# Layer norm, sliding attention and a Mish FFN on one core: additions ahead of the attention step, fixed PSUM banks, an interleaved start

## The chip, the core and the metric

The kernel runs on one core of a Trainium2 chip. The metric is the device time of one execution in microseconds. TensorE (PE) multiplies, VectorE (DVE), ScalarE (ACT) and GpSimd (POOL) do the elementwise work, SyncE (SP) issues the DMAs. Results of matmuls land in PSUM, of which the kernel holds eight banks of 128 x 512 fp32 values, four named h and four named out; everything else lies in SBUF, and what does not fit there is parked in DRAM.

## The reference

The input x has 2048 tokens of 576 features; all is fp32.

```python
xn = layernorm(x)
q, k, v = split(xn @ wqkv)              # 32 heads of 18
idx = pos - 2 * arange(8)               # each token sees 8 tokens, 2 apart, none behind the start
attn = softmax(where(idx >= 0, q . k[idx] / sqrt(18), -1e9))
o = (attn . v[idx]) @ wo
h = xn @ w1 + b1                        # 4608 hidden columns
return x + o + (h * tanh(softplus(h))) @ w2
```

Attention and FFN both read xn, and both are added to x.

## The kernel before, in words

**Two halves, products by seven.** The tokens go in two halves of 1024 (`hf`), each in two blocks of 512 (`b`) of four tiles of 128 tokens. Every fp32 operand of a matmul is split into a high and a low part, and a product is three matmuls (high x high, high x low, low x high). The FFN's first layer is computed transposed, 36 chunks of 128 hidden columns in 18 quads (`q`): a quad is a 2 x 2 block product, two token blocks by two chunks, done with seven block products and sums of blocks instead of eight products. In half 1 the first layer of quads 0 to 8 feeds a second layer that is also done by seven products (`p_item`, L847); all other quads use plain chunks of the second layer (`m2_pair`, L755, or `m2_cols`, L868), 24 matmuls on 288 columns each, four chunks per quad.

**A quad's six parts** (`m1_part`). Parts issue products of six matmuls on 512 columns (`prod`, L657) and remainders of two (`rest`, L663). There are three banks at a time: h1, h2 and h3, all from one pool tag of four buffers ("h"), which are handed out in turn. Part 0: a product into h1; ACT copies it to SBUF as c11 (`take`, L691); a product and a remainder into h2; DVE adds h2 to c11 (L702), ACT does Mish (L703) and the cast to the high part (L708), and GpSimd subtracts for the low part (L709): this is the activation A11. Part 1: a product into h3. Part 2: a product on top of h1, copied to c21. Part 3: a further product and a remainder on top of h1, copied to c22, which is added to h3 for A22. Part 4: a product and a remainder into h3, added to c21 for A21. Part 5: a product and a remainder on top of h1, read directly for A12. The other work of the "h" banks is the transposes of the first tiles (L77), the q, k, v items (L349, 15 matmuls on 432 columns for 128 tokens), the z items, which are the same work done by seven products in half 1 (L447), and the output projection (L1056).

**The order of the work.** Every engine executes its instructions in the order in which the program issues them. The program builds `plan`, a list of slots: q, k, v items, first-layer parts, second-layer chunks, output parts. In the FFN a quad has ten slots: six parts, and the four chunks of the quad before in between. Every slot has background work (`bg`: loads, casts, sums of weights, layer norm of later tiles), put there by `before(slot, fn)`. What must close a part (addition, Mish, cast, low part) is put on a list, `pend`, and is emitted in the next slot. When the plan is emitted, each slot gives out `first` (exponentials that an attention step of the slot before has ordered), then `bg`, then `held` (the closings of the slot before), then its own matmuls:

```python
    for i, (fns, bg, _) in enumerate(plan):
        first, soon[:] = soon[:], []
        held, pend[:] = pend[:], []
        for fn in first + bg + (fns + held if i == at["m", 0, 1, 0] else held + fns):
            fn()
```

**Attention** runs beside all this on GpSimd and DVE, as a generator of 72 steps per half (plus one to flush), which are spread over the slots. Heads go in pairs of groups; for a pair there are four steps with a query-key multiplication (L534, GpSimd, two instructions), one step with the softmax (maximum, difference, and the exponential on ACT, L559, one slot later), and four steps with a value multiplication (L572, GpSimd, two instructions), the first of them behind sum, reciprocal and product on DVE (L565). The reduction of a step's product (L539 or L578, DVE) is emitted at the head of the next step. A step is one function in the `bg` of its slot, the last of that list. Which slots get a step follows from planned costs: `PART` gives the cost of each part of a quad, `US` that of other slots, `rate` a density for each stretch of the plan (from `marks`), and a step is placed each time when the sum of cost times density passes a further 1/146 of `total`. In most quads only some of the ten slots may hold a step (`ok`).

**The start.** `prologue` takes tile 0 and tile 1 through the layer norm: statistics on DVE (L114), root on ACT, one Newton step on DVE, normalisation on ACT (L182, with a bias nm that DVE computes at L172), transposes on PE, copy to the high part on ACT (L83) and low part on DVE. Casts of the first query, key and value weights (L1172) stand in between. Then `first_item` issues tile 0's fifteen matmuls, with the transposes of tile 1 after eleven of them, then tile 1's with tile 2's transposes after eight, then tile 2's with tile 3's after four, and tile 3's.

**The end.** The last quad's four chunks of half 1 (slots "p") are followed by 24 slots "o" of the output projection (L1056 and the additions L1060). The operands of the first output items are split beside the last chunks (`o_split`, L906, L934, L935).

## Time and profile before

| what | us |
|---|---|
| runs: median (lowest to highest) | 1123.66 (1123.63 to 1123.96) |
| span of the profiled execution | 1121.6 |
| PE busy | 1109.5 (99%) |
| PE weight loads busy | 1023.0 (91%) |
| DVE busy | 829.0 (74%) |
| GpSimd busy | 787.7 (70%) |
| ACT busy | 492.1 (44%) |
| share of PE in the chain of work that ended last | 89% |

The span is that of one execution under the profiler, from its first to its last record; the runs' time is taken from outside and contains a little more. Times in the rows are microseconds from the start of the span. A row of the timeline reads: start, duration, engine, line, operation, out<-in, shape, count, and in brackets the idle time of the engine just ahead of it with the instruction that ended it. A row of the waits reads: waiting group <- releasing group: total us, count, longest. A row of the groups reads: engine, operation and tiles with their count: lowest, median and highest duration in ns, the time of the first and of the last start, and the shape. In the row of a run of equal instructions ("x12") the duration is that of the whole run.

### The profile page before, as it was taken

What the parts mean: (1) busy time and instruction counts of PE and PEld (TensorE: products, weight loads), DVE (VectorE), ACT (ScalarE), POOL (GpSimd) and SP (SyncE); (2) the same over time, 40 slices, a digit from 0 to 9 for tenths busy, and PEclk for the clock granted to TensorE, in tenths of its full rate; (3) what the DMA queues carried; (4) which work ended last, traced back from release to release, by engine and by line L of the source; (5) the groups of instructions that cost most, each with busy time, mean ns of one, the idle gap of its engine ahead of it and who ended that gap; (6) DMA issues with size and microseconds to landing.
All of it is one profiled execution on the core that took longest, in us unless ns stands there. A gap on an engine that the chain in (4) does not pass through costs nothing.

```text
span 1121.6 us, 18415 instructions
## 1 busy us (share of the span) xinstructions
PE 1109.5 (99%) x6630; PEld 1023.0 (91%) x6630; DVE 829.0 (74%) x1351; ACT 492.1 (44%) x892; POOL 787.7 (70%) x639
## 2 busy tenths in 40 slices
PE   8999999999999999999999999999999999999998
PEld 7999899999999999899999889999999999999998
DVE  6368788888888888877655456687866677776876
ACT  5544645544554545455233355343433343443332
POOL 2488767767689687676788476665789878668632
PEclk9999999999999999999999999999999999999999
DMA  6899885868767849666596797655655477676463
GB/s 200 283 312 318 290 283 205 289 228 284 261 240 258 282 163 345 222 240 214 191 342 238 231 373 249 241 200 174 227 198 189 168 263 269 215 253 248 157 222 104
DMA packets 147487, 271.08 MB, mean 242 GB/s; under 512 B 30114, under 2 KB 86724, under 8 KB 147396
## 3 DMA queue, kind: packets, MB, share of 16 engines
q1 hardware_dynamic: 147396, 269.91, 69.2%
q8 instruction: 52, 0.85, 0.3%
q14 instruction: 39, 0.32, 0.1%
HBM read 160.39 MB, written 109.48 MB: 241 GB/s over the span
## 4 chain that ended last, share of the span: by engine, by line
PE 89%; DVE 4%; POOL 3%; DMA 2%; issue 1%; ACT 1%; DVEq 0%; POOLq 0%; SPq 0%
PE h L657 28%; PE po L755 19%; PE pq L349 11%; PE po L868 10%; PE po L847 7%; PE h L663 5%; PE o L1056 4%; PE z L447 2%; DMA acc<-in_x 1%; POOL accP L856 1%; DVE u L801 1%; POOL pr L534 0%; DVE accP L871 0%; POOL act L709 0%; DMA z_B<-kept_wq 0%
## 5 line engine op out<-in xcount | busy, mean ns | idle before, releaser
L755 PEld LDWEIGHTS po<-w,act 128*128 128x128 f32 x1728 | 236.4, 188 | 7.5 <-DVE acc L759 1.7
L755 PE MATMUL po<-w,act 128*128 128x288 f32 x1728 | 240.8, 295 | 1.4 <-DVE acc L759 1.2
L534 POOL TENSOR_TENSOR pr<-q,kv 128x576 f32<-128x576 f32 x128 | 195.7, 1553 | 18.7 <-DMA q<-q_d 16.9
L572 POOL TENSOR_TENSOR pv<-L,kv 128x576 f32<-128x576 f32 x128 | 174.3, 1461 | 38.7 <-DVE L L565 20.9
L709 POOL TENSOR_TENSOR act<-c,act 128x512 fp32r<-128x512 f32 x81 | 107.1, 1322 | 128.4 <-ACT act L708 125.5
L759 DVE TENSOR_TENSOR acc<-po,acc 128x288 f32<-128x288 f32 x288 | 120.4, 450 | 31.6 <-PE po L755 30.2
L349 PE MATMUL pq<-wq,xt 128*128 128x432 f32 x672 | 136.2, 361 | 1.8 <-ACT xt L83 1.8
L868 PEld LDWEIGHTS po<-w,act 128*128 128x128 f32 x960 | 131.1, 188 | 3.7 <-DVE accP L871 0.4
L868 PE MATMUL po<-w,act 128*128 128x288 f32 x960 | 133.8, 295 | 0.2
L349 PEld LDWEIGHTS pq<-wq,xt 128*128 128x128 f32 x672 | 125.0, 188 | 8.7 <-ACT xt L83 2.7
L703 ACT ACTIVATE c<-c,b1c 128x512 f32<-128x512 f32 x81 | 58.7, 724 | 132.9 <-DVE c L702 132.6
L657 PE MATMUL h<-xt,t 128*128 128x512 f32 x432 | 110.6, 391 | 0.9 <-DVE c L702 0.8
L657 PE MATMUL h<-S,t 128*128 128x512 f32 x432 | 110.4, 391 | 0.0
L691 ACT COPY c<-h 128x512 f32<-128x512 f32 x81 | 47.4, 586 | 136.5 <-PE h L663 78.3
L578 DVE TENSOR_REDUCE og<-pv 128x144 f32<-128x1152 f32 x64 | 85.9, 1343 | 25.4 <-POOL pv L572 25.4
L657 PE MATMUL h<-xt,wa 128*128 128x512 f32 x432 | 104.0, 390 | 0.0
L657 PEld LDWEIGHTS h<-xt,wa 128*128 128x128 f32 x432 | 80.9, 188 | 16.9
L871 DVE TENSOR_TENSOR accP<-po,accP 128x288 f32<-128x288 f32 x160 | 69.6, 454 | 36.1 <-PE po L868 34.5
L847 PEld LDWEIGHTS po<-pw,u 128*128 128x128 f32 x672 | 92.4, 188 | 2.9 <-DVE u L801 0.5
L847 PE MATMUL po<-pw,u 128*128 128x288 f32 x672 | 94.2, 296 | 0.3 <-DVE u L801 0.3
L539 DVE TENSOR_REDUCE L<-pr 128x64 f32<-128x1152 f32 x64 | 85.8, 1341 | 11.2 <-POOL pr L534 11.1
L657 PEld LDWEIGHTS h<-xt,t 128*128 128x128 f32 x432 | 79.0, 188 | 16.1 <-DVE c L702 1.1
(231 smaller groups left out, 1840.5 us busy)
## 6 DMA issues: line engine op xcount, KB each, us to landing
kv<-kv_d SPq DMA_DIRECT2D x64, 396.0 KB, 5.2
kept_t<-t SPq DMA_DIRECT2D x36, 512.0 KB, 5.3
t<-kept_t SPq DMA_DIRECT2D x36, 512.0 KB, 5.4
rw<-in_w SPq DMA_DIRECT2D x36, 320.0 KB, 4.6
kept_wa<-wa SPq DMA_DIRECT2D x18, 640.0 KB, 3.5
kept_w<-w SPq DMA_DIRECT2D x20, 576.0 KB, 4.8
wa<-kept_wa SPq DMA_DIRECT2D x18, 640.0 KB, 6.1
w<-kept_w SPq DMA_DIRECT2D x20, 576.0 KB, 4.5
```

The source lines that it names most:

```text
L349: nc.tensor.matmul(pq[:, 0:432], XT[:, xi, tok], wt[wi][:, hl, 0:432], start=i == 0, stop=i == len(seq) - 1)
L534: nc.gpsimd.tensor_tensor(out=pr[:, x:x + hh], in0=q[:, j0 + x:j0 + x + hh, None, :].to_broadcast([P, hh, W, CU]), in1=win(kt, 0, CU, j0 + ...
L539: nc.vector.tensor_reduce(L[:, k, j0:j0 + hj].rearrange("p j w h -> p (j w h)"), pr.rearrange("p j w (h d) -> p (j w h) d", h=2), axis=AX, ...
L572: nc.gpsimd.tensor_tensor(out=pr[:, x:x + hj].rearrange("p j d w -> p j w d"), in0=L[:, k, x:x + hj, :, h:h + 1].to_broadcast([P, hj, W, DH]),
L578: nc.vector.tensor_reduce(og[:, :, c0:c0 + DH], pr, axis=AX, op=ALU.add)
L657: nc.tensor.matmul(ph, wt[:, wl, wk * P:(wk + 1) * P], X[:, xs, :], start=first and i == 0, stop=last and i == len(seq) - 1, skip_group_ch ...
L709: nc.gpsimd.tensor_tensor(out=a[:, 1, :], in0=t, in1=a[:, 0, :].bitcast(F32), op=ALU.subtract)
L755: nc.tensor.matmul(po, acts[hf, q, b, j][:, al, tok], done["w2", hf, 2 * q + j][:, wl, c * HC:(c + 1) * HC], start=i == 0, stop=i == 5)
L759: nc.vector.tensor_tensor(out=t, in0=po, in1=t, op=ALU.add)
L847: nc.tensor.matmul(po, units[e, k, qq][:, al, tok], w[:, qq, wl, :], start=i == 0, stop=i == 5)
L868: nc.tensor.matmul(po, acts[hf, q, b, j][:, al, tok], done["w2", hf, 2 * q + j][:, wl, c * HC:(c + 1) * HC], start=i == 0, stop=i == 5)
L871: nc.vector.tensor_tensor(out=t, in0=po, in1=t, op=ALU.add)
```

## The change

1. **Banks with fixed roles.** The tag "h" with four buffers becomes h1 (two buffers), h2 and h3 (one each). Named banks of a quad, a z item or an output item always take their own; other users go round in the order h1, h2, h1, h3.
2. **A sum in PSUM** (`seeded`, quads from 2 in half 0 and from 3 in half 1, 31 in all). Part 0 is only the product into h1, which ACT copies into the bank h2 and not into SBUF. Part 1 is h3's product, then h2's product and remainder on top of that copy. DVE's addition for A11 goes, and Mish reads the bank. The planned costs of parts 0 and 1 are exchanged.
3. **Half 1, quad 0.** The last two matmuls of h2's product, its remainder and the closing of A11 move from part 0 to behind part 3's copy c22.
4. **Order inside a slot.** The attention step is no longer part of `bg`; it comes behind the closings (`held`), and behind it come the low parts on GpSimd (`lows`), which were part of the closing. In part 0 of a seeded quad the order is `bg`, the slot's own matmuls, `first`, closings, step, low parts. The old exception for part 0 of quad 1 in half 0 goes.
5. **The start.** Single tiles are normalised on DVE (one tensor_scalar that subtracts and multiplies), nm goes. The items of tiles 0 and 1 are interleaved: eleven matmuls of tile 0, transposes of tile 1, then matmuls of both in turn, with the transposes of tile 2 ahead of the last four. Copies come ahead of low parts, and the casts of weights 2 to 4 behind tile 0's copies. Tile 3's transposes stand in tile 2's item after eight matmuls.
6. **Attention in fewer slots.** `total` ends at the first of the last four chunks and not at the third output item, so steps move by none to four slots to the front. The last steps stood in slots 421, 423, 425 and 427 (query-key), 428 (softmax), 429 to 432 (value) and 433 (flush), where 428 to 431 are the last four chunks and 432 is the first output slot; now they stand in 418, 421, 423 and 425, 427, 428 to 431 and 432.

```diff
@@ -62 @@
-    warm = ps.tile([P, 512], F32, tag="h", bufs=4, name="warm")
+    HT = ("h1", "h2", "h1", "h3")
+    hturn = [0]
+
+    def h_tile(name, n=None):
+        if n is None:
+            tag = HT[hturn[0] % 4]
+            hturn[0] += 1
+        else:
+            tag = f"h{n}"
+        return ps.tile([P, 512], F32, tag=tag, bufs=2 if tag == "h1" else 1, name=name)
+
+    warm = h_tile("warm")
@@ -81 (transpose_split) @@
-        nc.vector.tensor_sub(dst[:, 5:5 + KT, col:col + P], tav, hi.bitcast(F32))
...
+        def low_part():
+            nc.vector.tensor_sub(dst[:, 5:5 + KT, col:col + P], tav, hi.bitcast(F32))
+            nc.vector.tensor_sub(hr[64:P], tbv[64:P], hr[64:P].bitcast(F32))
         nc.scalar.copy(hr, tbv)
-        nc.vector.tensor_sub(hr[64:P], tbv[64:P], hr[64:P].bitcast(F32))
+        return low_part
@@ -165 (ln_newton, ln_norm) @@
-            nc.vector.tensor_scalar(m, g["mv"][:, 0, 0:1], r, -1.0, op0=ALU.mult, op1=ALU.mult)
...
-        nc.scalar.activation(xn[:, 0:D], accs[0][n], AF.Identity, bias=g["nm"][:, i, :], scale=g["rs"][:, i, :])
+        if g["k"] == 1:
+            nc.vector.tensor_scalar(xn[:, 0:D], accs[0][n], g["mv"][:, i, 0:1], g["rs"][:, i, :], op0=ALU.subtract, op1=ALU.mult)
+        else:
+            nc.scalar.activation(xn[:, 0:D], accs[0][n], AF.Identity, bias=g["nm"][:, i, :], scale=g["rs"][:, i, :])
         nc.gpsimd.tensor_copy(xn[:, D:D + 64], xn[:, KT * P:D])
@@ -507 @@
-    pend, soon = [], []
+    pend, soon, lows = [], [], []
+
+    def flush_lows():
+        for fn in lows:
+            fn()
+        lows.clear()
@@ -648 (bank, prod, mish) @@
-        cur[n] = ps.tile([P, TB], F32, tag="h", bufs=4, name=f"h{n}_{hf}_{q}")
+        cur[n] = h_tile(f"h{n}_{hf}_{q}", n)
...
+            if i not in some:
+                continue
...
+    seeded = lambda hf, q: q >= (2, 3)[hf]
...
-            nc.gpsimd.tensor_tensor(out=a[:, 1, :], in0=t, in1=a[:, 0, :].bitcast(F32), op=ALU.subtract)
+            lows.append(lambda: nc.gpsimd.tensor_tensor(out=a[:, 1, :], in0=t, in1=a[:, 0, :].bitcast(F32), op=ALU.subtract))
@@ -717 (m1_part) @@
         if part == 0:
             prod(bank(hf, q, 1), wa, 0, X0, 0, 5, True, True)
+            if seeded(hf, q):
+                nc.scalar.copy(bank(hf, q, 2), cur[1])
+                return
             take(hf, q, "c11")
-            prod(bank(hf, q, 2), wa, 2, X0, 2, 7, True, False)
+            prod(bank(hf, q, 2), wa, 2, X0, 2, 7, True, False, range(4) if (hf, q) == (1, 0) else range(6))
+            if (hf, q) == (1, 0):
+                return
             rest(cur[2], wa, 4, X0, 4)
             mish(hf, q, 0, 0, cur[2], cur["c11"])
         elif part == 1:
             prod(bank(hf, q, 3), t1, 0, X1, 0, 5, True, True)
+            if seeded(hf, q):
+                prod(cur[2], wa, 2, X0, 2, 7, False, False)
+                rest(cur[2], wa, 4, X0, 4)
+                mish(hf, q, 0, 0, cur[2])
...
             take(hf, q, "c22")
+            if (hf, q) == (1, 0):
+                prod(cur[2], wa, 2, X0, 2, 7, True, False, range(4, 6))
+                rest(cur[2], wa, 4, X0, 4)
+                mish(hf, q, 0, 0, cur[2], cur["c11"])
@@ -1139 (add) @@
-        plan.append((list(fns), [], PART[tag[3]] if tag[0] == "m" else US[tag[0]]))
+        part = tag[3] ^ 1 if tag[0] == "m" and tag[3] < 2 and seeded(tag[1], tag[2]) else tag[-1]
+        plan.append((list(fns), [], PART[part] if tag[0] == "m" else US[tag[0]], []))
@@ -1178 (prologue, first_item) @@
-        first_cast(0, nc.gpsimd)()
+        wl = [first_cast(0, nc.gpsimd)]
         ln_newton(0)
+        wl.append(first_cast(1, nc.gpsimd))
+        ln_norm(0)
+        wl[0]()
+        wl[1]()
         ln_stats(1)
-        low1 = first_cast(1, nc.gpsimd)
-        ln_norm(0)
-        low1()
-        first_cast(2, nc.gpsimd)()
+        low_part = ln_transpose(0, 0, 0, True)
         ln_root(1)
+        for k in range(2, 5):
+            wl.append(first_cast(k, nc.gpsimd))
+        low_part()
         ln_newton(1)
-        ln_transpose(0, 0, 0)
-        first_cast(3, nc.gpsimd)()
         ln_norm(1)
-        first_cast(4, nc.gpsimd)()
+        for k in range(2, 5):
+            wl[k]()
         ln_stats(2)
+
+    def first_pair():
+        prologue()
+        wt = [done["wq", 0, k] for k in range(5)]
+        XT = XTs[0, 0]
+        stage[0] = (sb.tile([P, 2 * UQ, JB, CU], F32, tag="w2", bufs=4, name="kvs_0_0_0"),
+                    sb.tile([P, UQ, JB, CU], F32, tag="mn", bufs=5, name="qs_0_0_0"))
+        pq = [ps.tile([P, 512], F32, tag="out", bufs=4, name=f"pq_0_0_0_{jj}") for jj in range(2)]
+        hh = [(k, k, 0) for k in range(KT)]
+        lh = [(k + 5, k, 0) for k in range(KT)]
+        hl = [(k, k, 1) for k in range(KT)]
+        count = [0, 0]
+
+        def mul(jj, *seq):
+            for xi, wi, w in seq:
+                nc.tensor.matmul(pq[jj][:, 0:432], XT[:, xi, jj * P:(jj + 1) * P], wt[wi][:, w, 0:432],
+                                 start=count[jj] == 0, stop=count[jj] == 13, skip_group_check=True)
+                count[jj] += 1
+        mul(0, *hh, *hl[0:2], *lh)
+        low_part = ln_transpose(0, 0, 1, True)
+        ln_root(2)
+        low_part()
+        ln_newton(2)
+        ln_norm(2)
+        rem_copy(0)
+        rem_copy(1)
+        ln_stats(3)
+        mul(1, *hh, *hl[0:2])
+        mul(0, hl[2])
+        mul(1, *lh)
+        mul(0, hl[3])
+        mul(1, *hl[2:4])
+        low_part = ln_transpose(0, 0, 2, True)
+        ln_root(3)
+        low_part()
+        ln_newton(3)
+        ln_norm(3)
+        rem_copy(2)
+        for jj in range(2):
+            mul(jj, (4, 4, 0), (4, 4, 1))
+            qkv_out(pq[jj], *stage[0], jj)
 
     def first_item(n):
         if n == 0:
-            prologue()
-
-        def mid():
-            if n == 0:
-                ln_root(2)
-                ln_newton(2)
-            ln_transpose(0, 0, n + 1)
-            if n == 0:
-                ln_norm(2)
-                ln_stats(3)
-                ln_root(3)
-                ln_newton(3)
-            if n == 1:
-                ln_norm(3)
-        if n < JB - 1:
-            qkv_item(0, 0, 0, n, mid, (11, 8, 4)[n])
-        else:
+            first_pair()
+        elif n == 2:
+            qkv_item(0, 0, 0, n, lambda: ln_transpose(0, 0, 3), 8)
+        elif n == 3:
             qkv_item(0, 0, 0, n)
@@ -1479 @@
-             spot(1, 2, 0), spot(1, 2 * OC + 2, 0), spot(1, NP - 1, 0), at["o", 0, 0], at["o", 2, 0]]
-    rate = (1.15, 0.4, 0.5, 0.8, 1.15, 1.3, 1.2, 0.8, 1.5, 0.8, 0)
+             spot(1, 2, 0), spot(1, 2 * OC + 2, 0), spot(1, NP - 1, 0), at["p", 1, NP - 1, 1, 0]]
+    rate = (1.15, 0.4, 0.5, 0.8, 1.15, 1.3, 1.2, 0.8, 1.5, 0.8)
...
-    total = T[at["o", 2, 0]]
+    total = T[at["p", 1, NP - 1, 1, 0]]
...
-        before(k, lambda hf=hf: next(att[hf], None))
+        plan[k][3].append(lambda hf=hf: next(att[hf], None))
@@ -1530 @@
-    for i, (fns, bg, _) in enumerate(plan):
+    early = {at["m", hf, q, 0] for hf in range(NH) for q in range(NP) if seeded(hf, q)}
+    for i, (fns, bg, _, steps_) in enumerate(plan):
         first, soon[:] = soon[:], []
         held, pend[:] = pend[:], []
-        for fn in first + bg + (fns + held if i == at["m", 0, 1, 0] else held + fns):
+        held, fns = held + steps_ + [flush_lows], list(fns)
+        for fn in bg + fns + first + held if i in early else first + bg + held + fns:
             fn()
```

The remaining lines of the diff put `h_tile` in the place of the old allocation of an "h" bank.

More of the change, by code (lines that the diff above doesn't have):

```diff
@@ L891, in o_split @@
             if early:
-                od["t"] = [ps.tile([P, 512], F32, tag="h", bufs=4, name=f"ot{k}_{p}") for k in range(3)]
+                od["t"] = [h_tile(f"ot{k}_{p}") for k in range(3)]
             else:
@@ L1047, in wo_part @@
         if part == 0:
-            od["h"] = [ps.tile([P, 512], F32, tag="h", bufs=4, name=f"o{n}_{p}")[:, 0:HC] for n in (1, 3, 2)]
+            od["h"] = [h_tile(f"o{n}_{p}", n)[:, 0:HC] for n in (1, 3, 2)]
         h1, h3, h2 = od["h"]
```

41 lines of the change are left out of this document (27 added, 14 removed).

## The prediction

> **What bounds the kernel now.** First the page, its span and the busy share of TensorE (PE).
>
> ```profile
> span 1121.6 us, 18415 instructions
> ...
> PE 1109.5 (99%) x6630; PEld 1023.0 (91%) x6630; DVE 829.0 (74%) x1351; ACT 492.1 (44%) x892; POOL 787.7 (70%) x639
> ```
>
> TensorE is busy in all but 12 us. The median of the runs, 1123.66 us, lies 2.06 us above this span; I leave those 2.06 us as they are. So the view of the waits comes second, for PE alone: all that this engine waited for, with the total, the count and the longest.
>
> ```profile
> PE pq L349 <- ACT xt L83: 1.8, 2, 1.1
> PE warm L67 <- POOL ident masks.py:199: 1.3, 1, 1.3
> PE o L1056 <- DVE y L1060: 1.3, 2, 0.7
> PE po L755 <- DVE acc L759: 1.2, 1, 1.2
> PE ta L77 <- ACT xn L182: 0.9, 1, 0.9
> PE h L657 <- DVE c L702: 0.8, 1, 0.8
> PE h L657 <- ACT rt L691: 0.7, 1, 0.7
> PE po L847 <- DVE u L801: 0.3, 1, 0.3
> ```
>
> These add up to 8.3 us, ten waits. The change adds or removes no matmul, so no more than 8.3 us is to be won, and 1.3 of it stands before anything that the change touches. Is the rest of PE's time dense? The chain of work that ended last gives one FFN quad, 50 matmuls on 512 columns and 96 on 288.
>
> ```profile
> 188.83 2.72 PE h L657 x12
> 193.36 3.18 PE po L755 x24
> ...
> 212.91 2.72 PE h L657 x12
> ```
>
> 2.72/12 = 0.227 us and 3.18/24 = 0.1325 us; 50 x 0.227 + 96 x 0.1325 = 24.07 us. The quad takes 212.91 - 188.83 = 24.08. The FFN's steady state has nothing to give. Each edit is therefore priced by what it does to the ten waits, and by new waits that it makes.
>
> **The sum in PSUM: 0.** In 31 quads (q from 2 in half 0, from 3 in half 1) the 128x512 copy of bank h1 goes into bank h2 and the addition on VectorE (DVE) goes.
>
> ```profile
> L691 ACT COPY c<-h x81: 572/587/602, 102.5 to 1028.0; 128x512 f32<-128x512 f32 x81
> L702 DVE TENSOR_TENSOR c<-h,c x81: 676/691/694, 111.6 to 1032.9; 128x512 f32<-128x512 f32 x81
> ```
>
> DVE is spared 31 x 0.691 = 21 us, none of it on PE's path. New is that PE waits for the copy: between h1's last matmul and h2's first lie six matmuls of h3, 1.36 us. I reckon 0.2 us until the copy sees h1 done, 0.59 for it and 0.05 back: 0.5 us to spare. No row shows a copy that ends in PSUM; from below it could be a little faster than 0.587, from above twice that, which just uses up the 0.5. I take 0.59, the same read and width. In these slots the copy is issued ahead of the exponential and of the last Mish, so only casts of weights stand before it. Fixed roles cost nothing here either: h3 is freed by an addition two slots ahead of its next use.
>
> **The start: +0.1.** The first weights and tiles, from the timeline.
>
> ```profile
> 6.24 0.21 DVE L172 TENSOR_SCALAR nm<-mv,rs 128x1 f32<-128x1 f32 x1
> 6.55 0.87 ACT L182 ACTIVATE xn<-acc,nm,rs 128x576 f32<-128x576 f32 x1 [0.18 <-ACT wq L1172]
> 8.72 0.57 ACT L83 CAST xt<-ta 128x512 fp32r<-128x512 f32 x1
> 9.34 2.45 PE L349 MATMUL pq<-wq,xt 128*128 128x432 f32 x11 [1.11 <-ACT xt L83]
> 10.76 0.82 DVE L114 BATCH_NORM_STATS2 st<-acc 128x6 f32<-128x288 f32 x2
> 18.29 0.65 PE L77 MATMUL ta<-ident,xn 128*128 128x128 f32 x4
> 455.42 0.75 DVE L257 TENSOR_TENSOR w<-rw,w 128x576 fp32r<-128x576 f32 x1
> ```
>
> The normalisation of 576 columns moves from ACT (0.87) to DVE, for which there is no row. Bounds: 0.21, a scalar operation of one column, and 0.87. I take 0.75, DVE's nearest row in width and memory (455.42). Then tile 0: normalised 6.24 + 0.75 = 7.0, transposed (0.65) 7.7, copied (0.57) 8.35: the first matmul at 8.4 instead of 9.34. But casts 2 and 3 now stand on ACT behind the copies and the root, and end near 9.3 and 9.8, so PE stops after two matmuls, 0.8 us in all. Ten matmuls later tile 1's transposes go out, and PE has nothing until their copy lands: 0.1 + 0.57 + 0.1 = 0.8. From there it is dense to item 2's eighth matmul. Tile 3's transposes wait for DVE, which has statistics (0.82 + 0.4), two low parts (1.0), Newton (0.6) and the normalisation (0.75) in a row behind tile 2's copy, whose end I put at 16.6: 19.2, against 18.29. By then four matmuls of 0.2 us more are done than before, so 19.2 - 18.29 - 0.8 = +0.1. With 0.21 it is -0.5, with 0.87 +0.3. The Trainium skill ("VectorE: DVE Perf Modes", section "The perf-mode tier table (the rule you actually need)") lets an fp32 tensor_scalar in SBUF run at twice the rate of a tensor_tensor; no row here shows one, and by it, an estimate of some 0.5 us, the start would come to -0.2.
>
> **Half 0, quad 1: +0.2.** The old loop let this quad's first part run ahead of the closing of quad 0; the new one doesn't (quad 1 isn't seeded).
>
> ```profile
> 118.40 0.72 ACT L703 ACTIVATE c<-c,b1c 128x512 f32<-128x512 f32 x1 [0.30 <-DVE c L702]
> 119.16 0.62 ACT L708 CAST act<-c 128x512 fp32r<-128x512 f32 x1
> 119.28 1.52 PE L657 MATMUL h<-S,t 128*128 128x512 f32 x6
> 130.27 1.65 PE L657 MATMUL h<-xt,t 128*128 128x512 f32 x6 [0.85 <-DVE c L702]
> ```
>
> Copy c11 now comes after this Mish and cast: 119.78 + 0.59 = 120.4, and the matmuls of 119.28, which overwrite h1, wait 1.1. At 130.27 PE waits 0.85 for a DVE chain that hangs on casts, not on PE; a later PE waits less there. 1.1 - 0.85 = +0.2; from 0 to +1.1.
>
> **Half 0, quad 15: -1.25.** The wait at L755.
>
> ```profile
> 458.56 1.35 DVE L578 TENSOR_REDUCE og<-pv 128x144 f32<-128x1152 f32 x1 [2.40 <-POOL pv L572]
> 463.90 1.54 DVE L759 TENSOR_TENSOR acc<-po,acc 128x288 f32<-128x288 f32 x4
> 464.40 3.46 PE L755 MATMUL po<-w,act 128*128 128x288 f32 x24 [1.25 <-DVE acc L759]
> ```
>
> DVE sat idle for 2.40 us with a reduction at its head and then came late to the chunk's additions. Softmax sum and reduction lay in neighbouring slots (part 5, then part 0). Worked through with the new total, the steps of this pair land on parts 4 and 5 with a chunk between: the 2.40 goes, and with it 1.25. If a reduction bunches there again: 0.
>
> **Half 1, quad 0: -0.7.** Four h2 matmuls, 0.91 us, move into the gap behind part 3, which a copy of 0.59 opens.
>
> ```profile
> 629.09 0.59 ACT L691 COPY ra<-h 128x512 f32<-128x512 f32 x1 [3.95 <-PE h L657]
> 636.10 1.66 PE L657 MATMUL h<-S,wc 128*128 128x512 f32 x6 [0.68 <-ACT rt L691]
> ```
>
> The place that they leave still has to cover the copy of 629.09: it ends at 629.68. By the 0.2 that I reckon until a copy sees its bank, PE began part 3 at 629.09 - 0.2 - 6 x 0.227 = 627.5 and now has ten matmuls before it needs the copy, to 629.8. Just covered. The 0.3 at L801 goes too, I assume: its chain starts with an addition behind attention reductions, and closings now come first: **-0.3**.
>
> **Attention one to four slots earlier.** In most slots DVE and GpSimd (POOL) have room. Two places have not.
>
> Column stage z of half 1, **+0.9**: GpSimd's multiplication, and the matmuls of part 3 of the first row.
>
> ```profile
> 572.81 1.30 POOL L608 TENSOR_TENSOR s_u<-xt,xt 128x512 f32<-128x512 f32 x1 [3.65 <-ACT L L559]
> 595.84 2.82 POOL L534 TENSOR_TENSOR pr<-q,kv 128x576 f32<-128x576 f32 x2
> 597.73 1.35 PE L447 MATMUL z<-z_B,S 128*128 128x432 f32 x6
> ```
>
> The reduction of 595.84's product moves from ahead of part 3 to ahead of part 2, where the addition that frees h1 for part 3 queues behind it (0.69 as at L702, 0.1 to PE). The product ends at 598.66. GpSimd idles 3.65 us earlier on, and a value step moved up fills about 2.2 of it: 596.5 + 1.34 + 0.79 = 598.6 against 597.73. Nothing filled: +3.0; all: 0.
>
> The end, **+1.8**: last chunks and the first output items.
>
> ```profile
> 1041.37 1.28 ACT L559 ACT_TABLE_LOAD   x1
> ...
> 1046.26 0.42 DVE L906 TENSOR_TENSOR s<-ot,a 128x256 f32<-128x256 f32 x1
> ...
> 1048.12 1.54 DVE L871 TENSOR_TENSOR accP<-po,accP 128x288 f32<-128x288 f32 x4
> ...
> 1055.30 1.30 POOL L935 TENSOR_TENSOR oS<-s,oS 128x512 fp32r<-128x512 f32 x1 [0.22 <-ACT oS L934]
> 1056.55 2.46 POOL L572 TENSOR_TENSOR pv<-L,kv 128x576 f32<-128x576 f32 x2
> ...
> 1058.29 1.86 PE L1056 MATMUL o<-wo,oS 128*128 128x288 f32 x12 [0.59 <-DVE y L1060]
> ```
>
> The exponential still waits behind the table load, to 1042.65, and ends some 0.45 later (1043.1); its sums (1.25) and the chunk's additions (1.54) take DVE to 1045.9, then the split's DVE work (1046.26 to 1048.12, 1.86): 1047.75. A reduction now stands ahead of the next additions: they begin 1049.1, not 1048.12: +1.0 for PE, which waits for their bank. The next chunk +0.3. Steps now come behind the slot's other work, so the last value multiplication stays behind L935 as before and ends about 1059; its reduction, one slot nearer, stands ahead of the first output addition: 1059 + 1.35 + 0.45 + 0.1 = 1060.9, where PE, by then 1.1 late, wants 1058.7: 2.2. That replaces the two waits at L1056 (1.3, or 1.6 with the pipeline's refill): 1.0 + 0.3 + 2.2 - 1.6 = about +1.8. From -1.6 (all product ready) to +3.
>
> **Sum:** 0.1 + 0.2 - 1.25 - 0.7 - 0.3 + 0.9 + 1.8 = +0.75: 1123.66 + 0.75 = 1124.4 us.
>
> **Rivals.** (1) Faster: GpSimd, with its idle time filled, is ahead of DVE in both places. Then z costs 0 and the end gives its 1.6: 0.3 - 2.25 - 1.6 = -3.55, **1120.1 us**. For it: POOL is 70% busy, and the reductions leave the output slots but for one. Against: the order on POOL at L935 is unchanged. (2) Slower: DVE reaches its reductions before GpSimd's products, in z and at the end. It decides from the point where a product ends later than DVE reaches it: z +3.0, the end +3.0: 0.3 - 2.25 + 6.0 = +4.05, **1127.7 us**. For it: 595.84 came late already. Against: the 3.65 us of idle time. (3) The copy into h2 is late by 0.3 us in each quad, once it ends 0.5 us later than I reckon: 31 x 0.3 = 9.3 + 0.75, **1133.7 us**. Against: ACT is 44% busy and its casts are early.
>
> **Chances.** Forecast 0.5, own range 1122 to 1126.5; (1) 0.22; (2) 0.22; (3) 0.06. A measurement of this kernel tells 0.2%, 2.25 us, from no change: 1121.4 to 1125.9 is "same". The forecast lies there with 0.44, and spills 0.03 below and above; faster 0.25, same 0.44, slower 0.31. The range takes in (1) and (2), 1119.5 to 1128.3, and leaves out (3) and the ends.
>
> **What would show it.** In the waits of PE: no wait at L755 and at L657 behind L691; at L1056 one wait over 2 us behind DVE; a wait near 1 us in L447 behind DVE; at L349 waits for wq casts; none at L657 for an ACT copy of h. A PE wait repeated in every quad would prove the forecast wrong, and so would a first matmul that starts early and an item 3 that ends a full microsecond earlier.

## The result and the profile after

The changed kernel takes 1130.26 us (median of 5 runs, 1129.78 to 1131.54) against 1123.66 (1123.2 to 1123.96): a ratio of 1.0059, 95% interval 1.0047 to 1.0071. It is 6.6 us slower, above the range that ended at 1128.3. The profiled execution spans 1128.0 us, 6.4 more than before, so the two traces can be set against each other place by place. First the page and the waits of PE (total, count, longest).

```profile
span 1128.0 us, 18307 instructions
...
PE 1111.1 (99%) x6630; PEld 1022.9 (91%) x6630; DVE 818.7 (73%) x1320; ACT 485.0 (43%) x888; POOL 792.1 (70%) x639
```

```profile
PE po L807 <- DVE acc L811: 2.6, 3, 1.1
PE z L477 <- DVE zqs L490: 2.4, 2, 1.5
PE o L1108 <- DVE y L1112: 1.9, 1, 1.9
PE warm L78 <- POOL ident masks.py:199: 1.3, 1, 1.3
PE h L694 <- DVE c L740: 1.2, 2, 0.8
PE pq L1266 <- ACT xt L93: 1.1, 2, 0.6
PE po L920 <- DVE accP L923: 0.9, 1, 0.9
PE ta L87 <- DVE xn L199: 0.7, 1, 0.7
PE z L477 <- ACT zqs L486: 0.6, 2, 0.3
PE po L899 <- issue: 0.3, 1, 0.3
PE pq L1266 <- ACT wq L1225: 0.3, 1, 0.3
PE h L694 <- ACT c L729: 0.2, 1, 0.2
```

Twenty waits, 13.5 us, where before had ten with 8.3. The lines have moved: L755 is now L807, L447 L477, L1056 L1108, L868 L920, L847 L899, L657 L694, L578 L613, L539 L574. The busy time of VectorE fell by 10 us only (829.0 to 818.7): 31 additions of 0.69 went, four normalisations of 0.58 came, and the other instructions took longer in sum (w at L284: 1287 ns on average instead of 1228).

The waits count idle time. A wait costs a little more than that (the 1.55 us at 602.40 are a loss of 1.71). So the table gives what PE lost at each place: the distance from the start of one matmul to the start of the next, less the pace of its width in the dense stretches (0.227 us for 512 columns, 0.197 for 432, 0.1325 for 288, 0.109 for 128), summed over all neighbours. Before it comes to 16.7 us, after to 23.0: the difference of 6.3 accounts for the span.

| stretch, us | place | before | after | moved by | forecast |
|---|---|---|---|---|---|
| 0 to 20 | start | 5.79 | 5.84 | +0.05 | +0.1 |
| 100 to 140 | half 0, quad 1 | 1.64 | 2.40 | +0.8 | +0.2 |
| 180 to 200 | half 0, quad 4, part 0 | 0.03 | 1.03 | +1.0 | 0 |
| 440 to 480 | half 0, quads 14, 15 | 1.64 | 1.13 | -0.5 | -1.25 |
| 520 to 540 | last chunks of half 0 | 0.11 | 1.50 | +1.4 | 0 |
| 580 to 620 | z stage | 0.18 | 4.08 | +3.9 | +0.9 |
| 620 to 680 | half 1, quad 0 | 1.73 | 0.46 | -1.3 | -0.7 |
| 680 to 800 | half 1, products by seven | 1.13 | 0.49 | -0.65 | -0.3 |
| 800 to 840 | the end of these | 0.59 | 1.14 | +0.55 | 0 |
| 1040 to 1120 | end | 2.89 | 3.96 | +1.1 | +1.8 |

What was to go did go, and the start came out near its forecast: tile 3's transposes begin at 19.03 against the 19.2 that the prediction puts there. The 6.4 us are six places that lose less three that gain, and more than half of them stand in the z stage.

**The z stage.** From the timeline of the changed kernel, first VectorE, then GpSimd, PE, ScalarE and SyncE's queue.

```profile
600.42 1.35 DVE L574 TENSOR_REDUCE L<-pr 128x64 f32<-128x1152 f32 x1 [2.71 <-POOL pr L569]
601.69 0.45 DVE L490 TENSOR_TENSOR zkv<-z,zkv 128x288 f32<-128x288 f32 x1
602.05 0.30 DVE L490 TENSOR_TENSOR zqs<-z,zqs 128x144 f32<-128x144 f32 x1
```

```profile
597.11 3.27 POOL L569 TENSOR_TENSOR pr<-q,kv 128x576 f32<-128x576 f32 x2
```

```profile
602.40 1.44 PE L477 MATMUL z<-z_B,S 128*128 128x432 f32 x6 [1.55 <-DVE zqs L490]
...
607.26 1.44 PE L477 MATMUL z<-zraw_T,S 128*128 128x432 f32 x6 [0.27 <-ACT zqs L486]
...
613.83 1.45 PE L477 MATMUL z<-z_B,S 128*128 128x432 f32 x6 [0.82 <-DVE zqs L490]
```

```profile
606.14 0.40 ACT L486 COPY zkv<-z 128x288 f32<-128x288 f32 x1 [7.50 <-DMA kv_d<-kvs]
```

```profile
596.04 0.53 SPq L615 DMA_DIRECT2D o_d<-og  x1
596.66 1.86 SPq L522 DMA_DIRECT2D kv<-kv_d  x1
598.61 0.39 SPq L392 DMA_DIRECT2D kv_d<-kvs  x1
```

The chain is the one of the prediction: VectorE sits 2.71 us at the head of its queue with a reduction whose product GpSimd ends at 600.4, and the two additions that free h1 stand behind it, to 602.35. PE goes on at 602.40. It happens again one row later, at 613.83. And a third thing: the step now stands one slot ahead of the store of the last q, k, v block, so that this store waits on SyncE behind the attention store and its loads until 598.61 (590.19 in before, whose PE is 2.7 us ahead here); ScalarE's copy at 606.14 needs its buffer and PE needs the copy.

**The two waits in half 0's chunks** at 446.65 and 535.87 look alike: the chunk's additions on VectorE come late behind an attention step that now stands in this slot. VectorE, then PE, at the first of them.

```profile
441.61 1.35 DVE L574 TENSOR_REDUCE L<-pr 128x64 f32<-128x1152 f32 x1 [1.59 <-POOL pr L569]
...
444.85 0.78 DVE L590 TENSOR_TENSOR L<-L,m 128x256 f32<-128x256 f32 x1
445.55 0.68 DVE L284 TENSOR_TENSOR t<-tt,t 128x512 fp32r<-128x512 f32 x1
446.15 1.54 DVE L811 TENSOR_TENSOR acc<-po,acc 128x288 f32<-128x288 f32 x4
```

```profile
446.65 2.52 PE L807 MATMUL po<-w,act 128*128 128x288 f32 x17 [0.75 <-DVE acc L811]
```

From 441.61 to 445.6 VectorE does a reduction, the mask, the maximum and the difference without a gap (the mask, ahead of 444.40, took 1.37 us here and 0.41 in before), then the low part of a weight sum; the additions of the chunk that PE began at 440.74 start at 446.15.

**The wait at 199.45** has another source. ScalarE, then VectorE, then PE.

```profile
191.06 0.57 ACT L764 COPY h<-h 128x512 f32<-128x512 f32 x1 [2.22 <-PE h L694]
191.65 1.28 ACT L594 ACT_TABLE_LOAD   x1
192.94 0.42 ACT L594 ACTIVATE L<-L 128x256 f32<-128x256 f32 x1
193.36 1.28 ACT L741 ACT_TABLE_LOAD   x1
194.66 0.69 ACT L741 ACTIVATE mn<-h,b1c 128x512 f32<-128x512 f32 x1
...
195.91 0.73 ACT L283 CAST wa<-rw 128x640 fp32r<-128x640 f32 x1
```

```profile
196.66 1.38 DVE L284 TENSOR_TENSOR wa<-rw,wa 128x640 fp32r<-128x640 f32 x1 [3.93 <-ACT wa L283]
197.97 1.06 DVE L330 TENSOR_TENSOR twT<-rw,rw 128x288 f32<-128x288 f32 x1
198.96 1.54 DVE L811 TENSOR_TENSOR acc<-po,acc 128x288 f32<-128x288 f32 x4
```

```profile
199.45 2.79 PE L807 MATMUL po<-w,act 128*128 128x288 f32 x19 [0.71 <-DVE acc L811]
```

The exponential comes behind the copy into h2, as the change puts it, and with it two table loads of 1.28, Mish and the cast of wa; VectorE idles 3.93 us for that cast with the additions queued behind it. In before Mish began at 193.16, 1.5 us earlier, of which 0.8 is the lag that quad 1 left. But the cast of wa ends only 1.0 us later than in before (196.6 against 195.6), so against PE it is late by 0.2. The larger part is VectorE itself. Its two subtractions behind the cast take 2.3 us from the first start to the additions, while GpSimd runs its own from 196.08 on; in before they took 1.2, and GpSimd stood idle from 195.9 to 197.2:

```profile
195.65 0.92 DVE L257 TENSOR_TENSOR wa<-rw,wa 128x640 fp32r<-128x640 f32 x1
196.48 0.45 DVE L303 TENSOR_TENSOR twT<-rw,rw 128x288 f32<-128x288 f32 x1
```

### The profile page after: what moved, and what is told of

Same layout as the page of the kernel before. It is cut to its first block, busy times and chain, and to the rows that moved or that the text cites. A ratio compares the mean times of both kernels' runs of the same rounds, so it can differ in the third digit from the quotient of the medians.

```text
span 1128.0 us, 18307 instructions
## 1 busy us (share of the span) xinstructions
PE 1111.1 (99%) x6630; PEld 1022.9 (91%) x6630; DVE 818.7 (73%) x1320; ACT 485.0 (43%) x888; POOL 792.1 (70%) x639
## 4 chain that ended last, share of the span: by engine, by line
PE 90%; POOL 4%; DVE 3%; ACT 2%; issue 1%; DMA 0%; DVEq 0%; POOLq 0%
PE h L694 29%; PE po L807 19%; PE po L920 11%; PE pq L380 9%; PE po L899 8%; PE h L700 6%; PE o L1108 5%; PE z L477 2%; POOL pv L607 1%; POOL s L643 1%; POOL pr L569 1%; PE warm L78 1%; PE ta L87 0%; PE pq L1266 0%; DMA kept_t<-t 0%
## 5 line engine op out<-in xcount | busy, mean ns | idle before, releaser
L807 PEld LDWEIGHTS po<-w,act 128*128 128x128 f32 x1728 | 236.4, 188 | 9.0 <-DVE acc L811 3.7
L807 PE MATMUL po<-w,act 128*128 128x288 f32 x1728 | 241.0, 295 | 2.6 <-DVE acc L811 2.6
L747 POOL TENSOR_TENSOR act<-c,act 128x512 fp32r<-128x512 f32 x56 | 73.7, 1316 | 112.4 <-ACT act L746 111.1
L920 PEld LDWEIGHTS po<-w,act 128*128 128x128 f32 x960 | 131.0, 188 | 4.1 <-DVE accP L923 1.1
L920 PE MATMUL po<-w,act 128*128 128x288 f32 x960 | 133.6, 295 | 0.9 <-DVE accP L923 0.9
L380 PE MATMUL pq<-wq,xt 128*128 128x432 f32 x644 | 129.6, 360 | 0.0
L380 PEld LDWEIGHTS pq<-wq,xt 128*128 128x128 f32 x644 | 120.3, 188 | 5.6
L694 PE MATMUL h<-xt,t 128*128 128x512 f32 x432 | 110.6, 391 | 1.2 <-DVE c L740 1.2
L694 PE MATMUL h<-S,t 128*128 128x512 f32 x432 | 110.6, 391 | 0.2 <-ACT c L729 0.2
L694 PE MATMUL h<-xt,wa 128*128 128x512 f32 x432 | 109.2, 390 | 0.0
L574 DVE TENSOR_REDUCE L<-pr 128x64 f32<-128x1152 f32 x64 | 85.9, 1342 | 28.9 <-POOL pr L569 28.8
L613 DVE TENSOR_REDUCE og<-pv 128x144 f32<-128x1152 f32 x64 | 85.8, 1342 | 29.0 <-POOL pv L607 28.9
L694 PEld LDWEIGHTS h<-xt,wa 128*128 128x128 f32 x432 | 80.9, 188 | 16.9
L899 PEld LDWEIGHTS po<-pw,u 128*128 128x128 f32 x672 | 92.2, 188 | 3.3 <-issue 0.5
L899 PE MATMUL po<-pw,u 128*128 128x288 f32 x672 | 94.2, 295 | 0.5 <-issue 0.3
L694 PEld LDWEIGHTS h<-xt,t 128*128 128x128 f32 x432 | 79.0, 188 | 16.7 <-DVE c L740 1.1
L694 PEld LDWEIGHTS h<-S,t 128*128 128x128 f32 x432 | 77.8, 188 | 13.5 <-ACT c L729 0.6
L729 ACT COPY c<-h 128x512 f32<-128x512 f32 x56 | 32.8, 586 | 125.5 <-PE h L700 75.0
```

The lines of the kernel that those rows point to most:

```text
L380: nc.tensor.matmul(pq[:, 0:432], XT[:, xi, tok], wt[wi][:, hl, 0:432], start=i == 0, stop=i == len(seq) - 1)
L574: nc.vector.tensor_reduce(L[:, k, j0:j0 + hj].rearrange("p j w h -> p (j w h)"), pr.rearrange("p j w (h d) -> p (j w h) d", h=2), axis=AX, ...
L613: nc.vector.tensor_reduce(og[:, :, c0:c0 + DH], pr, axis=AX, op=ALU.add)
L694: nc.tensor.matmul(ph, wt[:, wl, wk * P:(wk + 1) * P], X[:, xs, :], start=first and i == 0, stop=last and i == len(seq) - 1, skip_group_ch ...
L747: lows.append(lambda: nc.gpsimd.tensor_tensor(out=a[:, 1, :], in0=t, in1=a[:, 0, :].bitcast(F32), op=ALU.subtract))
L807: nc.tensor.matmul(po, acts[hf, q, b, j][:, al, tok], done["w2", hf, 2 * q + j][:, wl, c * HC:(c + 1) * HC], start=i == 0, stop=i == 5)
```

## The experiments

Theory S: the new slots of the attention steps (part 6) made most of the 6.4 us, those in half 0 and the z stage. Rivals: O, the order inside a slot (part 4); P, the sum in PSUM (part 2). The median of before lay between 1123.3 and 1125.0 when it was measured again, so times are given as ratios to the before measured beside them; places are read in the traces, by the measure of the table.

### Part 6 undone

```diff
-    total = T[at["p", 1, NP - 1, 1, 0]]
+    total = T[at["o", 2, 0]]
```

(with the two marks and the rate that go with it)

> Part 6 undone: total ends at the third output item again, all else as in the changed kernel. Theory S (the slots): the earlier attention steps made the waits at 446.65 (1.05 us), at 535.87 (1.4) and in the z stage (3.9 against 0.25), and took away the one at 464.40 (1.6). By it the z stage falls back to about 0.3, the two waits of half 0 go, the one of before at its L755 comes back, the end moves by under 1: 1130.3 - 1.05 - 1.4 - 3.6 + 1.6 = 1125.8 us, 1125 to 1126.6. Rival O (the order inside a slot): a step behind the closings starts its product on GpSimd later and so its reduction comes late, wherever it stands: z keeps over 2 us and the time stays above 1128.5.

Ratio 1.0026 (1.0016 to 1.0035), span 1124.6: 3.4 us less than the changed kernel. The z stage falls from 4.1 to 0.1, the waits at 446 and 535 are gone. S holds at these places, O's claim that z stays fails. Two things were missed. The wait at 464 did not come back (0.1 there). And new waits took their place: the end went from 4.0 to 5.4, and at 910.57 stands a wait that neither kernel has. VectorE, GpSimd and PE there:

```profile
903.97 6.17 DVE L1009 TENSOR_TENSOR raw_T<-raw_T,woh_T 128x576 fp32r<-128x576 f32 x1
910.07 1.54 DVE L923 TENSOR_TENSOR accP<-po,accP 128x288 f32<-128x288 f32 x4
```

```profile
903.92 5.61 POOL L569 TENSOR_TENSOR pr<-q,kv 128x576 f32<-128x576 f32 x4
```

```profile
910.57 1.72 PE L920 MATMUL po<-w,act 128*128 128x288 f32 x11 [1.87 <-DVE accP L923]
```

One subtraction of two SBUF operands took 6.17 us instead of the 1.29 that the same instruction took in before: it began 0.05 us behind the first of four GpSimd multiplications in a row and ended at 910.14, 0.6 us behind the last of them.

### Part 4 undone

```diff
-        held, fns = held + steps_ + [flush_lows], list(fns)
-        for fn in bg + fns + first + held if i in early else first + bg + held + fns:
+        for fn in first + bg + (fns + held if i == at["m", 0, 1, 0] else held + fns):
```

> Part 4 undone: steps in the background work ahead of the closings, low parts inside the closings, the exception for quad 1 of half 0 back, no early order in seeded quads; part 6 stays. Theory S: z keeps its 3.9 us and the waits at 446 and 536 stay; gone are only the wait at 199.45 (1.0, the exponential is ahead of the copy again) and that at 118 (0.8), while the copy into h2, now behind Mish and cast of the quad before, makes PE wait by some tenths in some quads: 1128.5 to 1132 us. Rival O: the z stage falls below 1 us and the time to about 1126.

Ratio 1.0169 (1.0155 to 1.0183), span 1143.5: 15.5 us worse than the changed kernel, far outside what S allowed. O fails all the same: z keeps 3.6 us. What it costs stands at two places. The copy into h2 waits behind exponential and Mish at quad 4 (5.3 us lost from 180 to 200), and at the end PE waits 7.7 us for a load (below, with the seventh experiment). So the new order is no cause of the loss in the z stage and at 446 and 535, and with parts 2 and 6 in place the old one is far worse. Two smaller places are the order's own (sixth experiment).

### Part 2 undone

```diff
-    seeded = lambda hf, q: q >= (2, 3)[hf]
+    seeded = lambda hf, q: False
```

> Part 2 undone: no quad is seeded, c11 goes to SBUF and is added on VectorE as before; with it goes the early order, and the planned costs of parts 0 and 1 are not exchanged, so a few steps move by a slot. Theory S: z keeps over 3 us; the wait at 199.45 goes (1.0): 1128.5 to 1130.5 us. Rival P (the sum in PSUM itself costs time, by PE's wait for the copy into h2): the time falls below 1127.

Ratio 1.0123 (1.0107 to 1.0138), span 1136.3. The wait at 199 goes, z keeps 4.1 (1.96, 1.55 and 0.46 at its three places), and P fails: without the sum in PSUM the span is 8.3 us longer, which also lies 7 us above the range of S. With VectorE's additions back, waits grow between 720 and 860 (5.4 us more than in the changed kernel: two behind VectorE, 0.73 at 739 and 0.86 at 745, and the largest, 2.29 at 838.67, behind a low part on GpSimd), and the flush falls so that PE waits 4.5 us for a load at the end. The wait of before at 464 is not there, although the additions are back; the last two experiments return to it.

### Parts 1, 3 and 5 alone

Parts 2, 4 and 6 undone by the three edits above.

> Parts 2, 4 and 6 undone together: what is left is the fixed banks, the split of quad 0 in half 1 and the new start. All that the theories dispute is away, so all of them expect the time of before less what quad 0 saves (1.0 us at 636) and with a start that is the same within 0.3: 1122.7 us, 1122 to 1123.5, with the waits of before at 464 (1.6) and 1058 to 1062 (1.6). If fixed banks cost anything it shows here as a wait of an h bank that before does not have.

Ratio 0.9996 (0.9987 to 1.0005), span 1121.5: no change, not the 1.0 us less that all theories expected. The wait at 636 is gone (0.17 lost from 620 to 640, 1.02 in before), but at 670.62 stands 1.0 where before has 0.19: PE arrives earlier at an addition of VectorE that comes no earlier (the difference of an attention step ahead of it took 1.25 us instead of 0.43). The fixed banks show no wait of their own.

### Old slots in half 0, new ones in half 1

The slots are placed twice, with the old and the new total, and joined:

```diff
+    cuts = [late_[n] if n < steps + 1 else soon_[n] for n in range(2 * steps)]
```

> The changed kernel, with the old slots for the attention steps of half 0 and the first of half 1, and the new slots for the rest of half 1. Theory S now says where: it is the slots of half 0 and of the z stage that cost, those of half 1's FFN do not. By it the waits at 446 (1.05), 535 (1.4) and in z (3.7 of 3.9) go, nothing comes back at 464, and the wait at 910 of the first experiment (2.2) is not there; the end keeps its 3.7 and the places at 118, 199 and 820 theirs: span 1128.0 - 6.1 = 1121.9 us, time within 0.1% of before. Rival O' (the order makes waits in half 1 with whichever slots): at least 2 us of new waits between 640 and 1040.

Ratio 1.0011 (1.0002 to 1.002), span 1123.7. The z stage has 0.4, nothing stands at 446, 535 or 464, nothing new between 640 and 800, and no wait at 910: S holds and O' fails. The span misses the forecast by 1.8 us, 1.6 of them at the end: after the 2.07 us lost at 1059.68, PE ran on at a granted clock of 0.62 (section on the hardware).

### The exponential ahead of the copy, and the exception of quad 1

```diff
-        for fn in bg + fns + first + held if i in early else first + bg + held + fns:
+        for fn in first + bg + fns + held if i in early else first + bg + (fns + held if i == at["m", 0, 1, 0] else held + fns):
```

> As the one before, with two edits to the order: in part 0 of a seeded quad the exponential goes ahead of the slot's copy into h2 again (the wait at 199.45, whose chain I read as exponential, Mish, cast of wa, DVE's low part, additions, all a table load late), and quad 1 of half 0 gets its old exception back (118 to 131: 2.37 us of waits against 1.66 in before). Expected: the wait at 199 goes (-1.0), the waits at 118 to 131 fall by 0.7, and where an exponential stands in such a slot the copy into h2 comes late by up to 0.5: span 1120.2 us, 1119.9 to 1121. Rival: the wait at 199 hangs on the chunk's place and not on the exponential, and stays.

Ratio 1.0 (0.9991 to 1.0009), span 1121.2, just above the range. The stretch from 100 to 140 falls from 2.42 to 1.71: this term is shown to be the exception. The wait at 199 is gone, as forecast; but 0.89 us stand now at 192.47, where PE waits for the copy into h2 behind the exponential, and the total of this place is the same. So this run doesn't show that the exponential made the wait at 199: VectorE's two subtractions took 1.39 and 1.08 us here too, and PE, 0.89 late already, arrives behind the additions that follow. What made the 1.0 us is in part argued from the traces.

### Steps ahead of the background work at the end

```diff
+        if i >= at["p", 1, NP - 1, 1, 0]:
+            bg, steps_ = steps_ + bg, []
```

> As the one before, with the steps ahead of the background work from the last quad's first chunk on, as they stood before the change. Theory E: the end waits (3.7 us) because the split of the first output items now stands ahead of the steps on VectorE and GpSimd, so that the last value multiplication starts behind the split's last subtraction. By it the last product ends some 3 us earlier against PE, and of 3.7 us about 1 stays: span 1117.5 us, 1116.8 to 1118.5; 0.3 to 0.45% below before. Rival: the reductions themselves are too many for VectorE beside the chunk additions; then the wait moves to the chunks and over 2.5 us stay.

Ratio 1.0072 (1.0059 to 1.0085), span 1130.1: a miss by 12.6 us, and neither side had its main cause. SyncE's queue, then PE:

```profile
1059.42 0.54 SPq L615 DMA_DIRECT2D o_d<-og  x1
1060.00 0.66 SPq L933 DMA_DIRECT2D o<-o_d  x1
```

```profile
1058.34 0.43 PE L1108 MATMUL o<-wo_r,ob 128*128 128x288 f32 x2
1065.99 1.09 PE L954 MATMUL ot<-ident,o 128*128 128x128 f32 x4 [7.23 <-DMA o<-o_d]
```

The last step issues the store of the attention's result on SyncE, which waits for the last reduction. Ahead of the background work of the first output slot, it stands ahead of the loads that the next output item needs, and they are issued at 1060.00 only. Theory E as put forward is not tested by this, as the wait covers it. The rival's sign is there, though: the loss in the last chunks grew from 1.03 to 2.48 us (1050.14, behind VectorE's additions), with a reduction ahead of the split that waited 1.35 us for GpSimd.

### The store one slot earlier, in the changed kernel

```diff
-    before(at["z", 0, 1], lambda: zq["send"]())
+    before(at["z", 0, 0], lambda: zq["send"]())
```

(and the end as in the kernel before)

> The changed kernel with its slots, and two edits at places far apart: the store of the last q, k, v block is issued one slot earlier (z stage), and the end as in the kernel before this one. Reading of the z stage: of its 3.9 us, 0.44 come from ScalarE's copy at 606.14, which waits for that store; the store was queued on SyncE behind an attention store. By it that wait goes, and the two waits on VectorE (1.7 and 1.0), which come from reductions ahead of additions, stay. If the z stage falls below 2 us, the store's place was the cause of the others too. The end falls as above.

One run, 1137.83 us, span 1136.1; the end has the load's wait again (12.7 us lost there). In the z stage the wait at 607 is gone as expected, but the rest did not stay: one addition wait of 0.63 at 602.61, none at 613, and new ones for loads of z operands (0.83 and 0.32 at 600) and for ScalarE (0.75 at 617.94); 3.1 us in all instead of 4.1. The place of a store on SyncE moves the whole stage; the split of the 3.9 us between store and reductions stays open.

### The joined version

Old slots in half 0, new in half 1, the exception of quad 1, and

```diff
-    seeded = lambda hf, q: q >= (2, 3)[hf]
+    seeded = lambda hf, q: q >= (2, 3)[hf] and (hf, q) != (0, 4)
...
+        if i in (at["p", 1, NP - 1, 0, 0], at["p", 1, NP - 1, 0, 1]):
+            bg, steps_ = steps_ + bg, []
```

> Old slots in half 0, new in half 1, old exception for quad 1; quad 4 of half 0, where an exponential meets the copy into h2, is not seeded; and the step stands ahead of the background work only in the last two of the four last chunks, so that the last value multiplication goes ahead of the split's last subtraction, while the last attention store stays behind the loads of the first output slot. The waits at 192 (1.0) and half of the 2.07 us ahead of the output items go, the 1.0 in the last chunks stays: 1121.2 - 1.0 - 1.1 = 1119.1 us of span, 1118.3 to 1120; 0.1 to 0.3% below before. If the store were late for the loads again, a wait of several us behind a DMA would stand at the second transposes of the output.

1120.94 us against 1124.17 for the before beside it: ratio 0.9973 (0.9963 to 0.9983), span 1119.2 as expected. It beats both kernels. Its waits of PE behind VectorE:

```profile
PE ta L87 <- DVE xn L199: 1.1, 2, 0.7
...
PE h L694 <- DVE c L740: 1.0, 2, 0.6
PE po L920 <- DVE accP L923: 0.9, 1, 0.9
PE o L1108 <- DVE y L1112: 0.6, 1, 0.6
```

Nothing is lost from 180 to 200, and the wait ahead of the output items falls from 1.9 to 0.6, with the last value multiplication ahead of the split's last subtraction and the store still behind the loads. That is theory E's point, at the place where it can be had.

### The sum alone, the order alone

Old slots in both; one keeps part 2, the other part 4.

> Old slots and old order, with the seeded quads (parts 1, 2, 3, 5). The wait of before at 464 (1.4 of 1.6 us) went with old and new slots, so either the additions saved on VectorE or the order took it away. If the additions: it is gone here. If the order: it is here. With the old order the copy into h2 stands behind exponential and Mish; at quad 4 of half 0 that costs 3.6 us (as in the second experiment): span 1121.5 + 3.6 + 0.3 = 1125.4 us, less 1.4 if the additions do it.

> Old slots, new order, no seeded quad (parts 1, 3, 4, 5). If the order takes the wait at 464 away it is gone here, else it is here. The end is as in the first experiment (4.7 us against 2.5 in before), since there the split stands ahead of the steps, and 118 to 131 costs 0.7 more: span 1121.5 + 2.0 + 0.7 = 1124.2 us, less 1.4 if the order does it; a wait in a place of half 1 may come as that at 910 did.

The sum alone: ratio 1.0063 (1.005 to 1.0077), span 1130.8 where 1124.0 was expected for the outcome that came; its four runs lie at 1129.4, 1129.4, 1132.2 and 1132.6, and the profiled one is the longest. The order alone: 1.0029 (1.0018 to 1.0041), span 1125.8 against 1124.2. In the first the wait behind VectorE's additions at 464 is gone (in its place 0.59 for the copy into h2), in the second it is there with 1.41 us. So with the old slots it is the additions saved by the sum in PSUM that take it away, and not the order. The new slots do it as well, without them: in the kernel with part 2 undone, which has the new slots and all the additions (and the new order, which alone leaves the wait there), the reduction at 455.35 starts without a gap and no wait stands at 464. The order alone loses at the end (5.2 us; before 2.9) and between 700 and 800 (2.6; before 1.1), the sum alone at its copy: 3.6 us at 195.59, 1.94 at 882, with 5.6 us of waits for L764 in all. ScalarE and PE at the first, and PE's granted clock in three stretches (the columns are span of the stretch, PE busy with its count, granted clock, DMA share, GB/s):

```profile
194.96 0.58 ACT L764 COPY h<-h 128x512 f32<-128x512 f32 x1
```

```profile
195.59 2.93 PE L694 MATMUL h<-xt,wa 128*128 128x512 f32 x6 [3.42 <-ACT h L764]
```

```profile
188.00:192.00 4.00, 4.00 (x19) 1.00 0.76 304
195.50:199.30 3.80, 3.71 (x9) 0.50 0.39 150
200.00:204.00 4.00, 4.00 (x25) 0.78 0.16 62
```

## Why the prediction was wrong

The step that failed is the sentence "In most slots DVE and GpSimd have room. Two places have not." and, in it, the size of the z term. The runs show 2.4 us in half 0's other slots, where the sum has nothing, and 3.9 in the z stage, where it has 0.9; with the old slots back there, both go (first and fifth experiment).

- **z stage, +0.9 forecast, +3.9 measured.** The mechanism was named (the reduction of the product that starts at 595.84 stands ahead of part 2's addition); three sizes were off. Against PE's part 2 the product began 1.45 us earlier, not 2.2 (598.88 - 597.11 = 1.77 ahead of it, 596.16 - 595.84 = 0.32 in before), and took 3.27 instead of 2.82. So the first row lost 1.7. The same happens in the next row, which the sum left out (1.0). And the step's DMAs were not counted: the store behind them came some 6 us later against PE on SyncE, at two waits of 0.4 for ScalarE, one of which follows from it. How the 3.9 divide between reductions and store stays open (eighth experiment). By the bound "nothing filled: +3.0" the loss was almost in sight.
- **Half 0's other steps: 0 forecast, +2.4 measured** (446 and 535). Only the pair that made the old wait at 464 was worked through; the pairs ahead and behind moved by up to four slots as well, one of them a softmax into a chunk's slot.
- **Half 0, quad 15: the -1.25 came**, and for the reason given: VectorE's idle 2.40 us ahead of the reduction are gone in the changed kernel, and the new slots take the wait away even with all additions in place. But it had a second reason that the prediction missed: with the old slots the saved additions alone remove it. "None of it on PE's path", said of these additions, was wrong.
- **The sum in PSUM: 0 forecast, right in itself.** The copy takes 0.570 us (L764, 31 times) against 0.59 reckoned, and in no quad of the changed kernel does PE wait for it: rival (3) fell. But "the copy is issued ahead of the exponential" was booked as a gain without its other side: at quad 4 the order around the copy costs 1.0. Behind the copy, the exponential moves two table loads, Mish and a cast of weights back; against PE that is 0.2 of it by the rows above, and the rest is VectorE's two subtractions, which ran beside GpSimd and took 1.1 longer. Without the sum at this quad nothing is lost there (0.03, joined version).
- **Quad 1, +0.2 forecast, +0.8 measured.** The wait for c11 came, with 0.34 and not 1.1 (120.38); one of 0.59 came ahead of it behind VectorE's addition (118.58), and stays when the exception is back; and the relief that was to come at 130 did not (0.98 there instead of 1.0).
- **Start, +0.1: right, with luck.** The tensor_scalar takes 0.58 us, between the bounds and below the 0.75 taken. The rule of the Trainium skill that was quoted ("VectorE: DVE Perf Modes", section "The perf-mode tier table (the rule you actually need)") points the right way but not so far: 0.58 is less than the 0.75 of a tensor_tensor of that width, by a factor of 1.3 and not 2. The terms listed for tile 3 add up to 16.6 + 1.22 + 1.0 + 0.6 + 0.75 = 20.2 and not to 19.2. The trace gives 19.03 because the statistics ran ahead of tile 2's copy (14.66 to 15.9) and not behind it.
- **Half 1, quad 0: -0.7 and L801: -0.3 forecast, -1.3 and -0.65 measured**, in the whole change. Alone, the quad's split gives nothing (fourth experiment).
- **The end, +1.8 forecast, +1.1 measured.** One wait of 1.9 ahead of the output items and one of 0.9 in the chunks, both as described; the prediction's own terms add up to +1.9.
- **800 to 840, 0 forecast, +0.55 measured.** A wait of 0.5 near 822 stands in most kernels of the study; its cause stays open.

Rival (1) fell with its first sentence, since GpSimd's product was not ahead of VectorE in the z stage. Rival (2) named the right engine and sign, and its +3.0 for z came near the 3.9; its +3.0 for the end did not come (+1.1), and it had nothing for half 0.

## What to carry to other kernels

When the slots of a background chain move, work through every slot that it enters, with all three of its queues: the reduction at the head of VectorE, the product on GpSimd and the DMAs on SyncE. A step that is early on one engine can put a store ahead of loads that the main path needs, and this was the dearest effect of the whole study (7 to 8 us). Undo the parts one by one and in halves of the plan: here the new slots cost some 6 us in half 0 and the z stage and nothing in the FFN of half 1, and two parts that each could have been the culprit made things worse when they were taken out.

## What the runs showed of the hardware

- **A wait can cost twice.** In the sum alone PE waits 3.42 us and then runs at a granted clock of 0.50 (the rows above): the eight matmuls from 196.18 on start 0.427 us apart instead of 0.227. The Trainium skill ("TensorE: Matmul & The Clock Gate", section "Part 1: The HAM clock gate (the "warmup" mystery)") says that an idle window of some 3.4 us halves the clock; the trace agrees. But a shorter wait did it too: the same 2.07 us lost at the output items left the clock at 1.00 in the changed kernel (1066 to 1070), with part 6 undone (1061 to 1065) and in the sixth experiment (1059 to 1063), and it was 0.62 behind it in one (1060 to 1064, old slots in half 0), at a price of 1.6 us. Why in that one is open.
- **VectorE beside GpSimd.** A subtraction of two SBUF operands lasted through four GpSimd products, 6.17 instead of 1.29 us. The Trainium skill ("SBUF — State Buffer", section "Who interferes with whom") says that a VectorE instruction with two SBUF inputs contends with a GpSimd instruction that reads SBUF, for a shared pair of ports under an exclusive lock. The trace agrees, with a hold through four GpSimd instructions in a row. In before the same subtraction began at 905.65 in such a row (904.90, four in 6.12 us) and ended at 906.94, 0.6 us behind the first product.
